# Raw second-layer weights loaded into the home of their low part and split there, one scratch for differences

## The chip, the cores and the metric

The kernel runs on one core of one Trainium2 chip. The metric is device time of one execution in microseconds (us), lower is better. TensorE (PE) multiplies, VectorE (DVE), ScalarE (ACT) and GpSimd (POOL) work on tiles in SBUF and on PSUM, and SyncE (SP) issues every DMA of this kernel in one queue, in the order of the program. Each engine takes its own instructions in order too; an instruction that waits holds all that stand behind it on its engine.

## What is computed

Three layers follow each other: causal attention with a decay, a gated layer with a layer norm (512 to 1024 to 512), and a squared-ReLU layer (512 to 2048 to 512). All is fp32.

```python
def reference(q, k, v, f, moe_w_in, moe_w_out, moe_g_ln, moe2_w_in, moe2_w_out):
    # batch 4, heads 8, tokens 576, head width 64
    cum = np.cumsum(np.log(np.clip(f, 1e-4, 1)), axis=-1)
    s = q @ k.T / 8 + cum[..., :, None] - cum[..., None, :]      # causal
    a = softmax(s) @ v
    x = a.reshape(2304, 512)
    h = x @ moe_w_in
    solu = h * softmax(h)
    x = (layernorm(solu) * moe_g_ln) @ moe_w_out
    h = np.maximum(x @ moe2_w_in, 0)
    return h * h @ moe2_w_out
```

## The kernel before

Products keep fp32 accuracy by splitting every operand into a high part (`hi`, rounded to fp32r) and a low part (`lo`, the difference), and running three matmuls: lo by hi, hi by lo, hi by hi. A split is one cast (`copy`, L376, L380 or L382 by engine: ACT, POOL, DVE) and one subtraction on DVE (`halves`, L1144).

Attention and the first layer take the time up to about 447 us of the profile. The second layer follows: tokens in blocks of 256, its 2048 hidden columns in eight pairs `p` of 256. A first block of 256 tokens is multiplied up by `half_up(p, ...)` (L1334), with weights `u0` to `u7` that `weightsh(p, ...)` loads and splits, into 32 homes `HU` of 128x512 (16 high, 16 low). All later blocks come in twos: `unit(b, p, ...)` (L1386) multiplies them up in seven products per pair (a Strassen scheme), and `step(blk, p, ...)` (L1487 to L1489) multiplies down, with weights of the second matrix that `weights2(p, ...)` loads and splits: per pair one piece of 256 columns (`a`) and three of 512 (`b`, `s`, `t`), each with a high and a low home. These homes are taken over from what the earlier stages leave: the first layer's weights `wih`, `wil`, `woh`, `wol`, the attention's `k1`, `k2`, `pt`, `e`, and small pieces of 256 (`ws`, `q3`, `qn`, `xc` and others). Many homes have two tenants in turn: `wil`, `k2`, `pt` and `e` hold weights of `half_up` first and weights of `step` afterwards.

Before the change, raw weights do not go to their homes. `load2` (L1158 to L1167) puts each into the next of six staging buffers `RAW` (`kn0`, `kn1`, `vn4`, `vn5`, `x`, `adj1`), and `halves` writes both parts into the homes. The same six buffers serve the token operands: `xload`, `xdiff` and `xsplit` of `x_block` (L1224, L1241, L1144) bring 512 tokens for the next units, and the last step of each block folds its output in them. The weights of the last pair come already split from DRAM (`w2s`, L1212).

A unit adds its products up with the help of a scratch of 128x256: it copies product 0 into it (`copy`), adds product 1, and then forms four sums from it (`add`, L1412). Before the change there are two scratches, `xw` and `maskb`, that units use in turn.

The order of all instructions is set by a planner, `Plan.lay`: each piece of work is a step with an engine, a cost, a priority (`prio`, a due time) and the buffer names that it reads and writes, and the planner lays them out as they become free. So a changed buffer changes the order on every engine. A load has the priority of its split less `AHEAD` (10 us). A home changes hands by `claim`, a step without cost that waits for the old tenant's last reader.

## Time and profile before

| | before |
|---|---|
| runs | 830.59, 824.18, 828.28 us; median 828.28 |
| profiled execution | 824.09 us, of it a span of 822.3 us |
| busy share of PE, DVE, ACT, POOL | 97%, 77%, 67%, 48% |
| DMA queue, share of 16 engines | 60.5% |

The profile is one execution. All times in the text are microseconds from the start of its span; 1.8 us of the execution lie around the span. A busy share is an average over the attention, the first and the second layer, which have different limits, so the stages are looked at one by one.

### The profile page before, as it was taken

The page shows a single profiled execution, that of the slowest core. Times are in us where ns is not written, and L with a number is a line of the kernel's source. Part 1 is how long each engine was busy: PE and PEld are TensorE (multiplying, and loading weights), DVE is VectorE, ACT ScalarE, POOL GpSimd, SP SyncE. Part 2 cuts the span into 40 slices and gives each one's busy share as a digit, 9 for nine tenths or more (in the row PEclk, how much of TensorE's full clock was granted, in tenths as well). Part 3 has the DMA queues.
Part 4 walks back from the last instruction along what each step waited for, and adds up shares of the span by engine and source line. Part 5 has one row for each costly group of instructions (what it writes and reads, how often), then busy time and mean ns, then how long its engine had stood idle before and what let it go on. Part 6 is the DMA issues. An engine that isn't in the chain of part 4 may idle for free.

```text
span 822.3 us, 19212 instructions
## 1 busy us (share of the span) xinstructions
PE 800.7 (97%) x6648; PEld 734.4 (89%) x6648; DVE 635.1 (77%) x1624; ACT 547.8 (67%) x1409; POOL 390.8 (48%) x539
## 2 busy tenths in 40 slices
PE   8899999999999999999999998999999999999997
PEld 7687777888888888888989998999999999999997
DVE  8898777878886667686658779779778867987776
ACT  6899988888797779899777676445335343533332
POOL 6467776767768777687777411021111121112110
PEclk9999999999999999999999999999999999999999
DMA  6643346657665554765557889896867767665401
GB/s 206 212 142 122 104 116 188 197 153 210 188 182 186 186 188 132 218 202 194 180 201 231 253 270 310 324 317 194 246 206 234 230 192 242 200 224 184 151 14 39
DMA packets 109665, 159.69 MB, mean 194 GB/s; under 512 B 12832, under 2 KB 52768, under 8 KB 109568
## 3 DMA queue, kind: packets, MB, share of 16 engines
q1 hardware_dynamic: 109568, 158.47, 60.5%
q8 instruction: 52, 0.85, 0.5%
q14 instruction: 45, 0.37, 0.2%
HBM read 121.65 MB, written 36.72 MB: 193 GB/s over the span
## 4 chain that ended last, share of the span: by engine, by line
PE 57%; ACT 3%; DVE 3%; issue 2%; DMA 1%; POOL 1%; DVEq 0%; POOLq 0%; ACTq 0%
PE pp L1386 9%; PE z L1386 9%; PE hp L1489 3%; PE hp L1488 3%; PE hp L1487 3%; PE z L1334 3%; PE pp L621 2%; PE z L567 2%; PE pp L811 2%; PE pp L812 2%; PE pp L813 2%; PE xo L641 2%; PE xo L1487 2%; PE xo L1489 2%; PE xo L1488 2%
## 5 line engine op out<-in xcount | busy, mean ns | idle before, releaser
L602 ACT ACTIVATE adj<-z,st 64x288 f32<-64x288 f32 (+9 forms) x192 | 95.1, 499 | 16.9 <-DVE st L588 15.9
L567 PE MATMUL z<-k,q 128*128 128x256 f32 (+17 forms) x384 | 90.0, 332 | 0.9 <-ACT adj L602 0.8
L588 DVE CUSTOM_DVE_ANT_0 z<-z,maskb 128x128 f32<-128x128 f32 (+8 forms) x144 | 65.2, 463 | 29.0 <-PE z L567 26.4
L621 PE MATMUL pp<-ident,adj 128*128 128x128 f32 (+1 forms) x480 | 76.6, 274 | 6.1 <-ACT adj L602 4.9
L812 PE MATMUL pp<-ln,wol 128*128 128x256 f32 x288 | 80.2, 278 | 0.0
L813 PE MATMUL pp<-ln,woh 128*128 128x256 f32 x288 | 80.1, 278 | 0.0
L1144 DVE TENSOR_TENSOR k<-adj,k 128x512 fp32r<-128x512 f32 x75 | 53.0, 706 | 33.8 <-POOL k L380 26.4
L376 ACT COPY pt<-pp 128x256 f32<-128x256 f32 (+5 forms) x169 | 67.2, 418 | 17.2 <-PE pp L621 16.1
L621 PEld LDWEIGHTS pp<-ident,adj 128*128 128x128 f32 (+1 forms) x480 | 50.6, 140 | 30.8 <-ACT adj L602 18.9
L380 POOL TENSOR_SCALAR k<-adj 128x512 fp32r<-128x512 f32 x39 | 24.3, 623 | 89.1 <-PE xo L1489 31.8
L734 POOL TENSOR_TENSOR free<-free 128x256 uint32<-128x256 uint32 x64 | 51.2, 807 | 31.0 <-DVE free L728 24.2
L567 PEld LDWEIGHTS z<-k,q 128*128 128x128 f32 (+3 forms) x384 | 54.9, 177 | 7.5 <-ACT adj L602 3.8
L641 PE MATMUL xo<-pt,vn 128*64 128x128 f32 (+1 forms) x960 | 61.1, 268 | 0.5 <-ACT pt L376 0.3
L860 PE MATMUL hp<-wih,xl 128*128 128x512 f32 x144 | 60.3, 419 | 0.8 <-ACT hp L899 0.8
L641 PEld LDWEIGHTS xo<-pt,vn 128*64 128x64 f32 x960 | 49.0, 137 | 11.3 <-issue 6.3
L861 PE MATMUL hp<-wil,xh 128*128 128x512 f32 x144 | 56.7, 394 | 0.2 <-DVE wil L738 0.2
L862 PE MATMUL hp<-wih,xh 128*128 128x512 f32 x144 | 56.7, 394 | 0.0
L812 PEld LDWEIGHTS pp<-ln,wol 128*128 128x128 f32 x288 | 54.4, 189 | 0.5
L813 PEld LDWEIGHTS pp<-ln,woh 128*128 128x128 f32 x288 | 54.2, 188 | 0.0
L1097 POOL TENSOR_TENSOR free<-free 128x256 f32<-128x256 f32 x64 | 52.5, 820 | 2.9 <-DMA w2f<-free 0.2
L1386 PE MATMUL z<-wol,k 128*128 128x256 f32 x384 | 52.5, 278 | 0.1
L1386 PE MATMUL pp<-wol,ln 128*128 128x256 f32 x384 | 51.9, 278 | 0.0
(597 smaller groups left out, 2686.3 us busy)
## 6 DMA issues: line engine op xcount, KB each, us to landing
k<-w2u SPq DMA_DIRECT2D x96, 256.0 KB
ln<-w2u SPq DMA_DIRECT2D x96, 256.0 KB
w2u<-free SPq DMA_DIRECT2D x56, 256.0 KB
kn<-in_k_dram SPq DMA_DIRECT2D x32, 256.0 KB
free<-in_moe_w_out_dram SPq DMA_DIRECT2D x32, 256.0 KB
free<-in_moe_w_in_dram SPq DMA_DIRECT2D x32, 256.0 KB
q<-w2u SPq DMA_DIRECT2D x32, 256.0 KB
w2f<-free SPq DMA_DIRECT2D x49, 128.0 KB
```

The lines of the kernel that those rows point to most:

```text
L376: nc.scalar.copy(dst(), src())
L567: nc.tensor.matmul(dst, lhsT=ql[0:r, p, 0:m], rhs=rhs, start=(g == 0), stop=(g == 1))
L588: nc.vector.tensor_tensor_reduce(out=z, in0=z, in1=maskb[0:m, o : o + e - a], scale=1.0, scalar=st[0:m, 0:1] if y else 3e38, op0=ALU.add, ...
L602: nc.scalar.activation(out=adj[0:m, c[1] : c[2]], in_=Z[c[0]][0:m, 0 : c[2] - c[1]], func=AF.Exp, bias=st[0:m, low : low + 1], scale=-1.0, ...
L621: nc.tensor.transpose(at(sk)[:, (c - g) * m : (c - g + 1) * m], adj[0:m, zc : zc + P], ident[0:m, 0:m])
L641: nc.tensor.matmul(XO[own[j], g // 2, off : off + m], lhsT=VN[vslot[b, c]][:, (g + j) * D : (g + j + 1) * D], rhs=PT[(s - h + g + j) % NPT ...
L812: nc.tensor.matmul(px, lhsT=wol[:, fc, w], rhs=hi, start=False, stop=False)
L813: nc.tensor.matmul(px, lhsT=woh[:, fc, w], rhs=hi, start=False, stop=(fc == KF - 1))
L860: nc.tensor.matmul(HP[:, c], lhsT=XL[i][:, cc, :], rhs=wih[:, cc, w], start=(cc == 0), stop=False)
L861: nc.tensor.matmul(HP[:, c], lhsT=XH[i][:, cc, :], rhs=wil[:, cc, w], start=False, stop=False)
L862: nc.tensor.matmul(HP[:, c], lhsT=XH[i][:, cc, :], rhs=wih[:, cc, w], start=False, stop=(cc == KC - 1))
L1386: nc.tensor.matmul(half(i), lhsT=l, rhs=r[:, c * TB : c * TB + TB], start=(j == start), stop=(j == 5), skip_group_check=True,)
```

## The change

Three things change. Each raw weight of the second layer is loaded into the home of its low part, cast from there into the home of its high part, and the low part is formed in place (`within` in the place of `load2` and the split); both homes are claimed 10 us of priority earlier, since the load needs one of them. The six staging buffers are left to the tokens and the outputs. `unit` has one scratch (`maskb`) in the place of two. The freed `xw` becomes the last small weight home, in the place of the end of `k11` (a last piece of 256 of `GS`), and its allocation stands a little earlier.

```diff
     new("q3", [640])
+    new("xw", [256])
...
     ident = new("ident", [P])
-    new("xw", [256])
...
-    GS = carve("k11", [512] * 5 + [256])
+    GS = carve("k11", [512] * 5)
...
-    small += GS[5:]
+    more("xw", 0, 1)
...
-    U2 = [carve(a, [256], F32)[0] for a in ("xw", "maskb")]
+    U2 = carve("maskb", [256], F32)[0]
...
-    turn = [0]
-
-    def load2(src, rk, n, prio):
-        ri = turn[0] % len(RAW)
-        turn[0] += 1
-        once(("raw", ri), RAW[ri], rk2(ri), prio)
+    def within(src, rk, hi, hk, lo, lk, n, prio):
 
         def fn():
-            dst = RAW[ri][0]()[:, 0:n]
+            dst = lo().bitcast(F32)
             nc.sync.dma_start(dst.rearrange("p (c x) -> p c x", x=256) if len(src.shape) == 3 else dst, src)
 
-        pl.add(dict(dma=LOAD2 * n / 512), fn, prio - AHEAD, rk, rk2(ri)[0 : n // 256])
-        return ri
+        pl.add(dict(dma=LOAD2 * n / 512), fn, prio - AHEAD, rk, [lk])
+        copy(n, hi, lambda: lo().bitcast(F32), prio, [lk], [hk], (), None, False)
+
+        def sub():
+            nc.vector.tensor_tensor(out=lo(), in0=lo().bitcast(F32), in1=hi().bitcast(F32), op=ALU.subtract)
+
+        pl.add(dict(dve=67 + 1.045 * n), sub, prio, [hk], [lk], port=True)
...
-                claim(HU[m], [hkeys[m]], prio)
+                claim(HU[m], [hkeys[m]], prio - AHEAD)
...
-                claim(W[nm + a], [("w2", p, nm + a)], prio)
+                claim(W[nm + a], [("w2", p, nm + a)], prio - AHEAD)
...
-        u2 = U2[n % 2]
-        uk = ("u2", n % 2)
-        once(uk, u2, [uk], prio)
+        uk = "u2"
+        once(uk, U2, [uk], prio)
```

In the order of instructions, lines of the changed kernel are two or three lower than before from L1170 on: `step` has L1484 to L1486, `unit` L1383, the adds to the scratch L1409. Its weight loads and weight splits are L1159 and L1165. The names give the tile that is written, the arrow what is read.

First the SP queue where the loads for `half_up` end. `w2d` are the raw weights of `half_up`, `w2f` those of `step`, `x2d` tokens. Before:

```order
L1164 DMA kn_50_4662<-w2d 128x512
L1164 DMA kn_50_4740<-w2d 128x512
L749 DMA w2d<-free_748 128x256
L1164 DMA vn_50_5380<-w2d 128x512
L1164 DMA vn_50_5425<-w2d 128x512
L749 DMA w2d<-free_748 128x256
L1164 DMA x_5434<-w2d 128x512
L1092 DMA w2u<-free_748 128x512
```

In the changed kernel:

```order
L1159 DMA pt_5396<-w2d 128x512
L1223 DMA kn_50_4673<-x2d 128x2x256
L749 DMA w2d<-free_748 128x256
L1223 DMA kn_50_4751<-x2d 128x2x256
L1159 DMA wil_5547<-w2d 128x512 x4
L749 DMA w2d<-free_748 128x256 x2
L837 DMA x2d<-xc_1416 128x256
L1092 DMA w2u<-free_748 128x512 x2
L1159 DMA wih_5648<-w2f 128x2x256 x3
```

The loads go to `pt` and `wil` now, the staging buffers `kn` take tokens, and four loads into `wil` stand together ahead of two stores of `w2d`.

Next DVE, where the splits of pair 4's weights (homes `wil`, after `half_up` is done with them) stand among the sums of the first two units and the split `k<-adj` that `step` of pair 2 reads. Before:

```order
L1144 TENSOR_TENSOR wil_5512<-vn_50_5425,wil_5512 128x512
L1412 TENSOR_TENSOR maskb_6172<-maskb_6172,pp_127 128x256
L1412 TENSOR_TENSOR ln1b_6082<-xw_6123,z_122 128x256 x2
L1144 TENSOR_TENSOR wil_5512<-adj_50_5282,wil_5512 128x512
L1144 TENSOR_TENSOR wil_5512<-kn_50_4662,wil_5512 128x512
L1412 TENSOR_TENSOR xl_50_5609<-maskb_6172,pp_125 128x256
L1412 TENSOR_TENSOR xl_50_5609<-xl_50_5609,pp_125 128x256
L1144 TENSOR_TENSOR wil_5512<-kn_50_4740,wil_5512 128x512
L1144 TENSOR_TENSOR k_50_5323<-adj_50_5620,k_50_5323 128x512
```

In the changed kernel:

```order
L1409 TENSOR_TENSOR maskb_6084<-maskb_6084,z_121 128x256
L1165 TENSOR_TENSOR woh_5909<-woh_5909 128x512
L1165 TENSOR_TENSOR wil_5547<-wil_5547 128x512
L1409 TENSOR_TENSOR ln1b_6072<-maskb_6084,z_122 128x256
L1409 TENSOR_TENSOR ln1b_6072<-ln1b_6072,z_122 128x256
L1165 TENSOR_TENSOR wil_5547<-wil_5547 128x512 x2
L1144 TENSOR_TENSOR ln1a_5939<-adj_50_5731,ln1a_5939 128x384
L1144 TENSOR_TENSOR k_50_5306<-adj_50_5667,k_50_5306 128x512
L1409 TENSOR_TENSOR ln1b_6072<-maskb_6084,z_122 128x256 x2
```

The splits of `wil` read no staging buffer any more. They still stand shortly ahead of `k<-adj`, and the second unit's sums in `maskb` stand behind the first unit's.

Last the SP queue where the loads of `step`'s weights end. Before:

```order
L1164 DMA kn_50_4662<-w2f 128x256
L1164 DMA kn_50_4740<-w2f 128x2x256
L1164 DMA x_5434<-w2f 128x256
L1164 DMA vn_50_5380<-w2f 128x2x256
L1164 DMA vn_50_5425<-w2f 128x2x256
L1164 DMA adj_50_5282<-w2f 128x2x256
L1164 DMA kn_50_4662<-w2f 128x2x256
L1164 DMA kn_50_4740<-w2f 128x2x256
L1164 DMA x_5434<-w2f 128x2x256
```

In the changed kernel:

```order
L1159 DMA woh_5909<-w2f 128x256
L1159 DMA free_5931<-w2f 128x2x256 x2
L837 DMA x2d<-xc_1416 128x256
L1159 DMA free_5931<-w2f 128x2x256
L1159 DMA woh_5909<-w2f 128x2x256 x4
L1372 DMA k_50_5306<-w2u 128x512
L1159 DMA wil_5547<-w2f 128x2x256 x3
L1372 DMA q_50_5367<-w2u 128x512
L1372 DMA ln_50_6088<-w2u 128x512 x3
```

Before, each load takes a staging buffer that an earlier load in the list had; now each goes to a home of its own.

## Rows read from the trace of the kernel before

**Rows 1.** The page's part 1: busy time, share of span, instructions.

```profile
PE 800.7 (97%) x6648; PEld 734.4 (89%) x6648; DVE 635.1 (77%) x1624; ACT 547.8 (67%) x1409; POOL 390.8 (48%) x539
```

**Rows 2.** Waits of PE over the span: total us, times, longest us.

```profile
PE pp L621 <- ACT adj L602: 4.9, 10, 1.3
PE xo L1487 <- DVE k L1144: 3.0, 2, 2.8
```

**Rows 3.** Stretches: length, busy PE, PEld, DVE, ACT, POOL; PE clock, DMA share, GB/s.

```profile
490.00:496.60 6.60, 6.60 (x57) 6.43 (x55) 6.09 (x14) 5.12 (x12) 0.00 (x0) 1.00 0.89 276
496.60:499.50 2.90, 0.15 (x3) 0.02 (x1) 2.38 (x6) 2.60 (x7) 0.62 (x1) 1.00 0.89 275
...
500.60:504.20 3.60, 3.60 (x20) 3.60 (x19) 2.87 (x9) 1.02 (x2) 1.92 (x2) 0.53 0.86 275
504.20:507.10 2.90, 2.61 (x21) 2.23 (x19) 2.46 (x6) 2.60 (x6) 0.17 (x1) 1.00 0.99 289
507.10:520.00 12.90, 12.90 (x108) 12.71 (x108) 11.35 (x32) 5.92 (x13) 0.00 (x0) 1.00 1.05 371
```

**Rows 4.** The chain that ended last, 491 to 500 us: start, us, what.

```profile
491.79 0.68 DVE woh L1144
...
492.50 4.83 DMA kn<-w2f
...
497.48 0.63 POOL wil L380
...
498.13 0.30 DVE wil L1144
...
498.74 0.70 DVE k L1144
...
499.48 0.38 PE xo L1487
```

**Rows 5.** Waits of the DMA queue (SPq), 440 to 510 us: total, times, longest.

```profile
SPq L1164 <- DVE q L1144: 3.9, 2, 2.7
SPq L1164 <- DVE k L1144: 3.8, 4, 1.8
SPq L1164 <- DVE wil L1144: 3.5, 4, 1.2
```

**Rows 6.** Timeline of PE: first layer's last read, then `half_up`'s first and last of `wil`.

```profile
442.33 0.40 PE L862 MATMUL hp<-wih,xh 128*128 128x512 f32 x1
...
450.74 0.88 PE L1334 MATMUL z<-vn,wil 128*128 128x256 f32 x6
...
452.14 2.32 PE L1334 MATMUL z<-vn,wil 128*128 128x256 f32 x18
...
468.93 0.88 PE L1334 MATMUL z<-vn,wil 128*128 128x256 f32 x6
```

**Rows 7.** Timelines of SP and ACT: a raw weight's load and its cast.

```profile
462.07 0.33 SPq L1164 DMA_DIRECT2D kn<-w2d  x1
...
465.74 0.62 ACT L376 CAST e<-kn 128x512 fp32r<-128x512 f32 x1 [2.32 <-DMA kn<-w2d]
```

**Rows 8.** Stretches as in rows 3, while the second layer's weights arrive.

```profile
440.00:460.00 20.00, 20.00 (x167) 19.61 (x166) 17.20 (x29) 15.68 (x35) 14.88 (x18) 1.00 0.78 244
460.00:480.00 20.00, 20.00 (x173) 20.00 (x173) 14.32 (x28) 12.43 (x29) 5.14 (x7) 1.00 0.81 255
```

**Rows 9.** The chain where two units start back to back: start, us, what.

```profile
570.71 2.84 PE pp L1386 x24
573.55 2.76 PE z L1386 x24
578.69 2.04 PE pp L1386 x18
585.49 2.04 PE z L1386 x18
```

**Rows 10.** Stretches as in rows 3, in the attention and first layer.

```profile
150.00:200.00 50.00, 49.78 (x402) 44.16 (x402) 38.61 (x106) 42.79 (x113) 35.93 (x48) 1.00 0.63 187
```

More of the change, by code (lines that the diff above doesn't have):

```diff
@@ L1174, in weightsh @@
         for c in range(2):
-            ri = load2(w2d[2 * p + c], [("w2d", 2 * p + c, z) for z in range(2)], 512, prio)
             for a in "hl":
@@ L1179, in weightsh @@
                 H2[p][f"u{c}{a}"] = HU[m]
-                claim(HU[m], [hkeys[m]], prio)
+                claim(HU[m], [hkeys[m]], prio - AHEAD)
             W = H2[p]
-            halves(
-                RAW[ri][0], rk2(ri), W[f"u{c}h"][0], ("w2", p, f"u{c}h"), W[f"u{c}l"][0], ("w2", p, f"u{c}l"), 512, prio
+            within(
+                w2d[2 * p + c], [("w2d", 2 * p + c, z) for z in range(2)],
+                W[f"u{c}h"][0], ("w2", p, f"u{c}h"), W[f"u{c}l"][0], ("w2", p, f"u{c}l"), 512, prio
             )
@@ L1199, in weights2 @@
                 W[nm + a] = again((small if n == 256 else large).pop(0))
-                claim(W[nm + a], [("w2", p, nm + a)], prio)
+                claim(W[nm + a], [("w2", p, nm + a)], prio - AHEAD)
             if p < KP - NPRE:
                 src = w2f[p, c[0]] if n == 256 else w2f[p, c[0] : c[0] + 2].rearrange("c p x -> p c x")
-                ri = load2(src, [("w2f", p, k) for k in c], n, prio)
-                halves(
-                    lambda ri=ri, n=n: RAW[ri][0]()[:, 0:n], rk2(ri)[0 : n // 256], W[nm + "h"][0], ("w2", p, nm + "h"),
+                within(
+                    src, [("w2f", p, k) for k in c], W[nm + "h"][0], ("w2", p, nm + "h"),
                     W[nm + "l"][0], ("w2", p, nm + "l"), n, prio,
@@ L1248, in x_half @@
             xsplit(g, 5 + g, prio)
-        turn[0] = 2
     def x_block(b, prio):
@@ L1352, in unit @@
         s1, s2 = (2 * b - 1, p), (2 * b, p)
-        u2 = U2[n % 2]
-        uk = ("u2", n % 2)
-        once(uk, u2, [uk], prio)
+        uk = "u2"
+        once(uk, U2, [uk], prio)
         def u2f():
-            return u2[0]()
+            return U2[0]()
         def half(i):
```

## The prediction

> **What bounds the kernel now.** I read the page's busy times first, then PE's waits, then the stretches in which they fall, the chain through the longest of them, and the waits of the DMA queue. PE is busy for 800.7 of the 822.3 us of the span [rows 1]. So 21.6 us of idle PE, and time lost to a low clock, are all that any change of order can win while the matmuls stay. PE's waits show where a piece of it lies that this change can reach: the waits of L621 on ACT belong to the attention, and the one long wait of the second layer is L1487 on the DVE split `k<-adj`, 2.8 us at its longest [rows 2]. In the stretches it stands at 496.6 to 499.5: PE is busy for 0.15 of 2.90 us [rows 3]. PE is full right before it (6.60 of 6.60) and from 507.1 on [rows 3].
>
> The chain says what was late there. The staging buffer `kn` is read by a split of `woh` from 491.79; as that ends, at 492.50, the next load into `kn` starts; it takes 4.83 us; POOL casts it (0.63), DVE subtracts for `wil` at 498.13, and only then comes DVE to `k<-adj` (0.70), for which PE starts at 499.48 [rows 4]. The weight in `wil` belongs to pair 4 and is not what PE wants; it merely stands ahead of pair 2's `k<-adj` on DVE. So the cause is a staging buffer that was free too late. The DMA queue shows the same from its side: weight loads wait for DVE splits that still read a staging buffer, 3.9, 3.8 and 3.5 us in the three longest groups [rows 5]. Meanwhile the DMA engines are not full: a share of 0.78 and 0.81 at 244 and 255 GB/s, against 1.05 and 371 GB/s at 507 to 520 [rows 8, 3].
>
> The gap has a price behind it. After it, PE's granted clock is 0.53 for 3.60 us, about the lower of its two levels (1.2 of 2.4 GHz), then back at 1.00 [rows 3].
>
> **The change part by part. Removed: the staging ring for weights.** What goes is the wait of a load on the split of an earlier load. Its worth is what PE lost: 2.90 - 0.15 = 2.75 us of gap, 3.60 x (1 - 0.53) = 1.69 us of low clock, and 2.90 - 2.61 = 0.29 us of the small wait behind it [rows 3], 4.73 us together. That all of it goes needs `wil`'s loads to be early by then. `half_up` reads `wil` last at 468.93, done at 469.81 [rows 6]; a load that then takes 4.83 us [rows 4] is there at 474.7, some 23 us before DVE came to it at 498.13 [rows 4]. In the new SP order these loads stand behind eight others into `woh` and `free`; at 256 KB each (2.1 MB) and the 255 GB/s of that time [rows 8] they take 8 us of the 23. In the order the splits of `wil` still stand ahead of `k<-adj`, so a late load would block DVE just as before; it is earliness alone that cures this.
>
> The work itself is the same: the same number of loads, of casts and of subtractions, at the prices of the old ones (0.63 for a cast, about 0.69 for a subtraction [rows 4]). That DVE reads and writes one tile costs no row anything; from both sides it lies between nothing and one more 0.69 per split, and I take nothing since the shape is the same.
>
> **Added: a load now waits for its home.** Before, a raw weight could lie in staging while its home was in use; now cast and subtraction wait for a load that starts only when the home is free. It matters where home and use are close together, at `wil`: PE reads the first layer's weights last at 442.33 + 0.40 = 442.73, and `half_up` wants `wil` at 450.74 and from 452.14 on [rows 6]. Four loads stand together. A raw weight took 465.74 - 462.07 = 3.67 us from the start of its issue to its cast [rows 7], 4.83 at the slowest [rows 4]; issues follow each other by about 0.4 (an issue takes 0.33 [rows 7]). So the first `wil` is there at 446.4 and split by 447.7. The third, with the casts one behind the other, is cast by 448.3 and split by 449.0; for the other work that ACT and DVE have there (15.68 and 17.20 of 20 us [rows 8]) I add the worth of two pieces, 1.3, which makes 450.3. The slack is 1.8 us against 452.14, and 0.6 with the slow load. I take nothing, and keep as the other end 3 us plus a clock dip of 1.69. The cover is PE's own work from 442.73 to 450.74, matmuls that need none of this.
>
> Here a rule of the Trainium skill speaks against the change. The page "Trainium Kernel Development and Optimization", section "Best Practices", says to double-buffer so that DMA overlaps with compute, and the change gives six staging buffers up. By that rule the loads at `wil` stand uncovered, and the time would be that of the second rival below; by the rows, other work of PE covers them, and the sum loses nothing.
>
> **Added: one scratch.** The second unit's copy waits until the first unit's last two sums are formed. Units mostly start after the one before has ended. Where two start back to back, the first (pp) has its second half from 578.69 to 580.73 and the next (z) its second half at 585.49 [rows 9]: 4.76 us for two sums, a copy and three sums. None of these is in my rows; the nearest is a split at twice the width, 0.69 [rows 4], and six of these make 4.1. It fits. There are six such places. Only at the first two units, near 485 to 495, does the new order bring the second unit's second half close behind the first's. I price this place at 0.4, between nothing and 1.4 (two pieces at 0.69).
>
> **Moved: three small splits** (`ws`, `q3`, `qn`) into the attention stage, since their homes are long free. Each has half the width of a split, so at most 0.63 + 0.69 us [rows 4], on ACT, POOL and DVE. By their neighbours in the order the first two fall into 150 to 200, where ACT and DVE work for 42.79 and 38.61 of 50 us and PE for 49.78 [rows 10]. Bounds: nothing, or the three in full, 4.0 us. PE there is bound by its own work, so I take 0.3; without that cover it would be the 4.0.
>
> **The sum.** 824.09 - 4.73 + 0.4 + 0.3 = 820.1 us against the profiled execution's 824.09, a change of -4.0. That execution is at the lower end of the runs (824.18 to 830.59); on the median of 828.28 the same change gives 824.2 us, 0.5% less. About 1% is what a measurement of this kernel can tell from no change.
>
> **First rival: the stall stays or only moves.** The four `wil` splits stand ahead of `k<-adj` still, and all loads go through one SP queue: if a load into `woh` waits for its home, the `wil` loads behind it wait too, and DVE again stands in front of PE. For it: the queue is in order, and DMA is full at 507 to 520 [rows 3]. Against it: from 440 to 480 there is a fifth of DMA left [rows 8]. It wins back nothing: 828.3 us, or 826 if only half of the 4.73 goes.
>
> **Second rival, on the other side: `wil` late for `half_up`.** Place: PE's L1334 on `wil` at 450.74 to 452.85. If the four loads land over 1.8 us later than priced, each further us is one of PE; and over some 2 us a clock dip of 1.69 is added, as behind the gap of 2.75 [rows 3]. It makes the kernel slower than before once it costs over 4.0, so at loads late by 1.8 + 2.3 = 4.1 us, which would be 7.8 us for a load. For it: the queue stands behind stores of `w2d` that wait for POOL; against it: neither load of the rows took over 4.83. At 6 us late: 824.2 + 4.2 + 1.7 = 830.1.
>
> **How the numbers follow.** Forecast 0.64: 824.2, its own range 820 to 827 with the scatter of medians. First rival 0.20: 826 to 829. Second rival 0.12: 828 to 834. The remaining 0.04 is for more, where PE's waits in the attention shrink with the new order: below 819. The range of 817 to 831 leaves out the far end of the second rival and some scatter. Over 1% faster is below 820.0: the last case and the low end of the forecast, 0.12. Over 1% slower is above 836.6: the far end of the second rival and a small part of the first, where the stall moves to a dearer place, 0.08. Within: 0.80.
>
> **What would show it.** Right: no PE wait on a DVE split near 497, no stretch at half clock up to 786, SP no longer waiting on DVE splits for weight loads, full PE from 440 to 500, and the units starting about 4 us earlier at equal work. The first rival shows as a wait of L1484 on `k<-adj` with a weight load behind it; the second as a wait of L1332 on a split of `wil` near 451. The scratch would show as a wait of L1383 on the copy into `maskb`, about 493; the small splits as more waits of L621 at 160 to 200. I am wrong if PE's busy time itself differs, or if the order's new sequence of units costs waits at places that were full.

## The result and the profile after

| | before | after |
|---|---|---|
| median of the runs beside each other | 825.53 us (823.82 to 830.59) | 816.48 us (815.5 to 821.4) |
| ratio, 95% interval | | 0.9889 [0.9852, 0.9926] |
| profiled execution, of it the span | 824.09, 822.3 us | 816.74, 814.9 us |

The change makes the kernel 1.1% faster (0.7 to 1.5% by the interval). The forecast was 824.2 us with a range of 817 to 831, so the gain is larger than forecast, and the time lies just below the range.

The page's part 1 of the changed kernel stands beside [rows 1]. PE's busy time itself fell by 4.2 us, with the same 6648 matmuls (the low clock that the sum priced at 1.69 us is in that, since PE counts as busy at it):

```profile
PE 796.5 (98%) x6648; PEld 730.9 (90%) x6648; DVE 636.8 (78%) x1626; ACT 544.4 (67%) x1405; POOL 392.2 (48%) x541
```

The waits of PE from 440 to 815 us (total us, times, longest) answer the second line of [rows 2]. The wait of `step` on `k<-adj` of 3.0 us is gone. The 0.7 that is left stands in the kernel before as well:

```profile
PE pp L1484 <- DVE k L1144: 0.7, 1, 0.7
```

The waits of the DMA queue from 440 to 510 us answer [rows 5]. Before, the longest group was a store (L749, held by POOL, 4.8 us), and the three next, those of [rows 5], were weight loads held by a DVE split. Now no weight load waits for a DVE split. One of the two longest groups is a weight load (L1159), for a home that PE still reads:

```profile
SPq L837 <- ACT xc L376: 4.3, 2, 3.1
SPq L1159 <- PE pp L938: 3.6, 1, 3.6
```

The stretches (columns as in [rows 3]) answer [rows 3, 8]. PE is full in every one, the clock is granted whole, and the transfers that were crowded behind the stall now come earlier: 365 GB/s at 480 to 500.

```profile
440.00:460.00 20.00, 20.00 (x163) 19.41 (x162) 15.87 (x30) 14.62 (x32) 13.04 (x15) 1.00 0.80 252
460.00:480.00 20.00, 20.00 (x175) 20.00 (x174) 15.27 (x29) 13.50 (x32) 6.06 (x8) 1.00 0.88 273
480.00:500.00 20.00, 20.00 (x177) 20.00 (x176) 17.83 (x34) 13.23 (x27) 5.82 (x8) 1.00 1.08 365
500.00:520.00 20.00, 20.00 (x177) 20.00 (x177) 15.41 (x43) 8.70 (x18) 1.75 (x3) 1.00 0.92 314
520.00:540.00 20.00, 20.00 (x178) 20.00 (x177) 15.21 (x42) 6.39 (x15) 4.13 (x7) 1.00 0.69 233
```

Two stretches of the kernel before show what these columns say beside the busy time. PE is busy for 20.00 of 20.00 us in both, at a clock of 1.00, but it starts 174 matmuls of the same size in the one and 179 in the other:

```profile
520.00:540.00 20.00, 20.00 (x174) 20.00 (x174) 14.85 (x42) 7.65 (x18) 2.36 (x4) 1.00 0.84 294
540.00:560.00 20.00, 20.00 (x179) 20.00 (x178) 15.92 (x39) 10.32 (x20) 4.16 (x6) 1.00 0.87 300
```

So there is a second piece of gain, inside busy time. The chain of the changed kernel where two units start back to back answers [rows 9], which had 2.84 and 2.76 us for the same 24 matmuls (`pp` and `z`). Here the 24 matmuls of the `pp` unit take 2.76:

```profile
564.53 2.76 PE pp L1383 x24
567.29 2.08 PE z L1383 x18
```

One measure carries the rest of this text: the time from PE's last start in the first layer (`hp<-wih,xh`, [rows 6]) to the start of the last unit's six `pp<-q` matmuls. Between the two lie the same matmuls in every kernel. From PE's timeline of before and, below it, of after:

```profile
782.03 0.88 PE L1386 MATMUL pp<-q 128*128 128x256 f32 x6
```

```profile
443.55 0.40 PE L862 MATMUL hp<-wih,xh 128*128 128x512 f32 x1
...
774.80 0.88 PE L1383 MATMUL pp<-q 128*128 128x256 f32 x6
```

That is 782.03 - 442.33 = 339.70 us before and 774.80 - 443.55 = 331.25 after. The attention and the first layer, which the change hardly touches, end between 442.3 and 444.3 in nearly all profiles with no relation to the edits, so the whole span says less than this difference does. Kernels for which no median is given below were run once, and have one profile.

| kernel | first layer's last read | last unit | between |
|---|---|---|---|
| before | 442.33 | 782.03 | 339.70 |
| before_again | 444.20 | 783.31 | 339.11 |
| e2_ring_one | 443.67 | 781.93 | 338.26 |
| e1_inplace_two | 442.98 | 776.65 | 333.67 |
| e4_tail_home | 443.73 | 777.43 | 333.70 |
| e5_head_home | 442.94 | 776.63 | 333.69 |
| e6_swap_home | 444.16 | 779.68 | 335.52 |
| e9_xw_above | 448.08 | 781.57 | 333.49 |
| e10_e_above | 443.63 | 776.38 | 332.75 |
| e7_wait_steady | 442.64 | 779.56 | 336.92 |
| e8_claim_late | 444.29 | 777.54 | 333.25 |
| after | 443.55 | 774.80 | 331.25 |
| after_again | 442.93 | 774.18 | 331.25 |
| e11_lower_above | 443.75 | 784.81 | 341.06 |
| e12_q_swap | 443.79 | 784.85 | 341.06 |
| e13_lower_z | 442.88 | 773.60 | 330.72 |
| e14_lower_pp | 443.79 | 774.75 | 330.96 |

### The profile page after: what moved, and what is told of

It reads as the page before. It is cut to its first block, busy times and chain, and to the rows that moved or that the text cites. A ratio compares the mean times of both kernels' runs of the same rounds, so it can differ in the third digit from the quotient of the medians.

```text
span 814.9 us, 19217 instructions
## 1 busy us (share of the span) xinstructions
PE 796.5 (98%) x6648; PEld 730.9 (90%) x6648; DVE 636.8 (78%) x1626; ACT 544.4 (67%) x1405; POOL 392.2 (48%) x541
## 4 chain that ended last, share of the span: by engine, by line
PE 56%; ACT 3%; DVE 3%; DMA 2%; issue 2%; POOL 1%; DVEq 0%; SPq 0%; POOLq 0%; ACTq 0%
PE z L1383 9%; PE pp L1383 9%; PE hp L1484 3%; PE hp L1486 3%; PE hp L1485 3%; PE z L1332 3%; PE pp L621 2%; PE pp L811 2%; PE z L567 2%; PE xo L1484 2%; PE xo L1486 2%; PE xo L1485 2%; PE pp L812 2%; PE pp L813 2%; PE hp L860 1%
## 5 line engine op out<-in xcount | busy, mean ns | idle before, releaser
L1144 DVE TENSOR_TENSOR k<-adj,k 128x512 fp32r<-128x512 f32 x72 | 50.5, 701 | 32.9 <-POOL k L380 24.9
L1383 PE MATMUL z<-wol,k 128*128 128x256 f32 x384 | 52.5, 276 | 0.0
L1089 POOL TENSOR_TENSOR free<-free 128x256 fp32r<-128x256 f32 x63 | 48.3, 781 | 8.4 <-ACT free L376 7.5
```

Source lines behind the costliest of these rows:

```text
L1383: nc.tensor.matmul(half(i), lhsT=l, rhs=r[:, c * TB : c * TB + TB], start=(j == start), stop=(j == 5), skip_group_check=True,)
```

## Experiments: which part of the change wins

No kernel below leaves out a part of the computation. Where a diff starts from the changed kernel, its minus lines are that kernel's; e2 starts from the kernel before.

**The kernel before once more, and the changed one once more.** Same files, to see the scatter of one profile.

> The kernel before, unchanged, profiled once more. If what the first profile showed belongs to the program, the gap near 497 us is 2.7 to 2.9 us again, the matmuls from 507 to 532 us stand 0.1175 us apart, and the slow stretches at pair 7 stand at the same places with 0.17 us each. If they are chance of one execution, they stand elsewhere or not at all.

The stall is there again, at `k<-adj` as in [rows 2], 2.4 us at its longest, and the measured stretch is 339.11 against 339.70.

> The changed kernel, unchanged, profiled and timed once more. If the pace belongs to the program, units start 16.36, 9.56 and 2.76 us apart again, with no stretch at 0.1175 us per matmul from 483 us on; the end of the first layer, 443.5 us in the first profile, may move by 1 to 2 us, as it did between two profiles of the kernel before (442.3 and 444.2).

The median is 815.97 us (815.19 to 817.59), the ratio 0.9892 [0.9858, 0.9927], and the stretch is 331.25 again. So differences of half a microsecond in this stretch between kernels can be read, as far as these two pairs go; in the kernels with the stall they can't quite. A short wait that comes in one kernel and not in another can cost more than that, as e8 and e9 show below, so it matters where in the stretch a difference lies.

**The ring alone taken away.** The changed kernel with two scratches and with the last small home back at the end of `k11`.

```diff
-    GS = carve("k11", [512] * 5)
+    GS = carve("k11", [512] * 5 + [256])
...
-    more("xw", 0, 1)
+    small += GS[5:]
...
-    U2 = carve("maskb", [256], F32)[0]
+    U2 = [carve(a, [256], F32)[0] for a in ("xw", "maskb")]
```

> The change's first part alone: weights are loaded into the home of their low part and split in place, but units keep two scratches in turn and the last small weight home stays at the end of k11. Theory A (the ring made the stall, the home at the end of k11 makes the slow stretches): no idle PE and no half clock between 485 and 510 us, and none of the long stretch at 0.1175 us per matmul that the kernel before shows from 488 to 532 us; but the stretches of some 43 matmuls at 0.1175 us in place of 0.1133 us that stand at pair 7 of each block of the kernel before (568 to 573 us, 607 to 612 us and so on, 0.17 us each) are still there, 6 or 7 of them, 1.0 to 1.2 us in all. Span 815.9 to 816.3 us against 814.9 of the changed kernel. Theory B (those stretches are left over from the disturbed start and go with the ring): 814.9 us and an even pace. Theory C (the scratch, not the ring, is what helps): a wait of 2 us or more near 497 us is left and the span is 820 us or more.

Measured: 818.64 us, ratio 0.9934 [0.9916, 0.9952], span 816.9, stretch 333.67. The stall and the low clock are gone; the ring alone (with the earlier claims, which e8 tests) is worth 339.4 - 333.67 = 5.7 us (339.4 is the mean of the two profiles of before). But pace is lost a little later. In two stretches of this kernel, PE starts 178 matmuls and then 169, with 0.06 us idle in the second:

```profile
500.00:520.00 20.00, 20.00 (x178) 20.00 (x177) 15.66 (x45) 7.40 (x17) 2.33 (x4) 1.00 0.92 312
520.00:540.00 20.00, 19.94 (x169) 19.73 (x168) 14.31 (x40) 8.03 (x18) 2.88 (x5) 1.00 0.75 249
```

The span is 0.6 to 1.0 us above what was expected: that stretch after the first pass of pair 7 was not foreseen.

**The ring kept, all the rest changed.** The kernel before with one scratch and the home in `xw`.

```diff
-    small += GS[5:]
+    more("xw", 0, 1)
...
-    U2 = [carve(a, [256], F32)[0] for a in ("xw", "maskb")]
+    U2 = carve("maskb", [256], F32)[0]
```

> The other two parts alone: the six staging buffers stay as in the kernel before, units have one scratch, xw is the last small weight home and stands a little lower. Theory A: the stall near 497 us stays with its low clock behind it and the slower pace of matmuls up to some 530 us; the slow stretches at pair 7 are gone, 1.0 to 1.2 us less than before: span 821.0 to 821.4 us. Theory B: stall and slow stretches both as before, 822.3 us. Theory C: no stall, below 818 us. The first units would show a wait on the copy into the one scratch near 490 us if the scratch costs what I took for it, 0.4 us.

Measured: 823.84 us, ratio 0.9994 [0.997, 1.0018], stretch 338.26. The wait of PE stands as before, with the lost pace behind it up to about 527. The low clock that was expected behind it did not come: the granted clock is 1.00 throughout, though the wait is longer (3.3 us against 2.8). Two waits near 504 and 506, 0.9 us each by the starts, are longer than in the kernel before instead. First the wait, then two stretches:

```profile
PE xo L1486 <- DVE k L1144: 3.9, 2, 3.3
```

```profile
500.00:520.00 20.00, 18.20 (x147) 17.59 (x148) 18.03 (x48) 11.39 (x24) 0.80 (x1) 1.00 0.94 329
520.00:540.00 20.00, 20.00 (x176) 20.00 (x175) 15.04 (x41) 8.58 (x19) 2.38 (x4) 1.00 0.86 303
```

So the two other edits are worth 1.1 us while the ring is there, and the ring is worth 338.26 - 331.25 = 7.0 with the other edits in. With e1 the pieces are not additive, and the next runs say why.

**The home alone put back.** The changed kernel, with the last small home at the end of `k11`.

```diff
-    GS = carve("k11", [512] * 5)
+    GS = carve("k11", [512] * 5 + [256])
...
-    more("xw", 0, 1)
+    small += GS[5:]
```

> The changed kernel with one thing undone: the last small weight home is the end of k11 again, and xw stays where it is but holds nothing. Theory A: the slow stretches at pair 7 come back, 1.0 to 1.2 us over the changed kernel, span about 816.0 us, with no other difference from 440 us on. Theory B: 814.9 us, pace of 0.1133 us per matmul throughout.

Measured: 819.62 us, ratio 0.994 [0.9912, 0.9968], stretch 333.70. Against e1 (333.67) the scratch costs 0.03 us, which is nothing. Against the changed kernel (331.25) the place of one home of 256 columns costs 2.45 us. PE's timeline shows where. Columns: start us, us, engine, line, out<-moving operand,stationary operand. This is pair 7's `step` in e4; the second row streams the weight from the end of `k11`:

```profile
562.06 0.28 PE L1484 MATMUL hp<-xc,ln1a 128*128 128x256 f32 x1
562.17 0.28 PE L1485 MATMUL hp<-k,ln1a 128*128 128x256 f32 x1
562.29 0.28 PE L1486 MATMUL hp<-xc,ln1a 128*128 128x256 f32 x1
562.41 0.28 PE L1484 MATMUL hp<-e,ln1a 128*128 128x256 f32 x1
```

And this is the same place in the changed kernel, with the weight in `xw`:

```profile
561.99 0.28 PE L1484 MATMUL hp<-xc,ln1a 128*128 128x256 f32 x1
562.10 0.28 PE L1485 MATMUL hp<-xw,ln1a 128*128 128x256 f32 x1
562.22 0.28 PE L1486 MATMUL hp<-xc,ln1a 128*128 128x256 f32 x1
```

A matmul of 256 columns starts 0.113 us after the one before. In e4, from the one that streams out of `k11` on, starts lie 0.1175 apart in the mean, and stay so for 51 or 63 matmuls, through the next unit (on `pp`) to the six `z<-q` of the unit behind it. The chain of e4 therefore has 2.84 us for the 24 matmuls of that `pp` unit, where the changed kernel has 2.76 (above):

```profile
566.11 2.84 PE pp L1383 x24
```

This costs 0.2 us per block. Six such blocks make 1.2. The other 1.2 lie in the block ahead of them, where the slower pace that begins with pair 7 at 521.9 lasts until about 547: 178 + 178 matmuls in 520 to 560 in the changed kernel against 170 + 176 in e4, 10 fewer at 0.113, which is 1.1. In that stretch PE also waits twice for DVE, too briefly for the list of waits (near 523.7 and 529.3, 0.38 us together). e1 and e5 have these waits too, the changed kernel has not; whether they prolong the slower pace is not shown. In e2 and in the kernel before, that stretch was slow anyway, behind the stall, so there the home is worth only the six blocks (1.15 measured). That is why the parts don't add up one by one.

## Experiments: what about the home

**The head of `k11` in place of its end.**

```diff
-    GS = carve("k11", [512] * 5)
+    GS = carve("k11", [256] + [512] * 5)
+    HEAD, GS = GS[:1], GS[1:]
...
-    more("xw", 0, 1)
+    small += HEAD
```

> The changed kernel with the last small weight home (pair 7's low part of 256 columns) at the beginning of k11 instead of in xw; the homes of the sums' high and low parts move up by one place in k11. Theory A1 (what matters is the place at the end of k11): the even pace of the changed kernel, 16.36 and 2.76 us from unit to unit, span about 815 us. Theory A2 (what matters is that the weight shares k11 with operands that DVE, ACT and POOL write all the time): slow stretches at pair 7 as with the end of k11, 2.84 in place of 2.76 us from a unit to the next there, 2.5 us more than the changed kernel, span about 817.5 us.

Measured: span 816.9, stretch 333.69, with the same slower pace at pair 7. It is not the end of that tile, nor a tile's last bytes.

**The low part of pair 3 there in place of pair 7's.**

```diff
-    GS = carve("k11", [512] * 5)
+    GS = carve("k11", [512] * 5 + [256])
...
-    more("xw", 0, 1)
+    small.append(small[7])
+    small[7] = GS[5]
```

> The changed kernel with two small weight homes exchanged: the end of k11 holds pair 3's low part, the third piece of ws holds pair 7's. Theory A1 or A2 (the home is what matters): the slow stretches move to pair 3 of each block and are gone at pair 7; their length and price there (0.2 to 1.2 us a block) depend on what resets the pace. Theory A3 (pair 7's place in the order matters, whatever its home): they stay at pair 7, 0.18 us each.

Measured: span 820.4, stretch 335.52. The slower pace moves with the home: it begins in pair 3's `step` now, pair 7 is even, and it lasts longer (0.44 us a block). In the chain of e6 the first `pp` unit of this row lies behind pair 3, and the second begins as the slower pace has ended:

```profile
586.33 2.84 PE pp L1384 x24
...
596.24 2.76 PE z L1384 x24
```

**`xw` kept as the home, but allocated where it stood before.** The order of instructions is that of the changed kernel on every engine; only the addresses differ.

```diff
-    new("xw", [256])
     ADJ = [new(f"adj{i}", [AW]) for i in reversed(range(NADJ))][::-1]
...
     ident = new("ident", [P])
+    new("xw", [256])
```

> The changed kernel with one thing undone: xw is allocated where it stood before, 12.7 KB higher in each partition; the order of instructions is the same on every engine. Theory P (a matmul pays when its moving operand lies in the same upper part of the memory as the stationary operands k10, k11, ln0, ln1a): if that part begins below 170 KB, slow stretches at pair 7 as with the end of k11, 2.84 in place of 2.76 us there and 9.65 in place of 9.56, 1.3 to 2.5 us more than the changed kernel. Theory A2 (sharing the tile k11 is what matters): the even pace of the changed kernel, 16.36 and 2.76 us, the same time from 444 us on.

Measured: stretch 333.49, 2.24 us more than the changed kernel, with one allocation moved and no instruction. The chain shows pair 7's unit at 2.84 again:

```profile
570.25 2.84 PE pp L1383 x24
```

But only 1.3 of the 2.24 us lie at pair 7, where `step` reads `xw` seven times in the stretch, at 0.17 to 0.23 each. The other 0.9 were lost before the first of these reads. From PE's timeline, a start that comes 0.14 us late, and the first read of `xw`:

```profile
498.49 0.28 PE L1486 MATMUL hp<-wih,ln1a 128*128 128x256 f32 x1
498.74 0.97 PE L1383 MATMUL pp<-wol,ln 128*128 128x256 f32 x6
...
529.31 0.28 PE L1485 MATMUL hp<-xw,ln1a 128*128 128x256 f32 x1
```

There PE waits for a sum on DVE, and behind it the slower pace holds until 518. Neither profile of the changed kernel has this wait, though the order is the same; e10 and e8, below, have it. DVE's split `ln1a<-adj` shortly before takes 0.97 us in e8, e9 and e10 and 0.55 in the changed kernel; why is open, and since e8 leaves all addresses as they are, the place of `xw` is not shown to be the cause. So the address is worth 1.3 us here, and that the whole comes near the 2.45 of e4 is chance.

(The whole span was 821.4, since in this profile PE's clock was granted at 0.93 over 100 to 200, in the attention, and the first layer ended at 448.08; this is why only the second layer is compared.)

In the program as built, `xw` lies at byte 158,144 of each partition in the changed kernel and at 170,880 in e9; `k11`, where the other kernels have the home, begins at 193,408. The stationary operands of `step` lie above 180,000 (`ln1a` at 216,960, `k10` at 182,144), and two other homes that it streams from lie lower (`wil` at 18,880, `e` at 121,792). The tiles allocated between the two places of `xw` move down by its 1,024 bytes in e9; in e10, below, those between move by 4,096.

**`e` allocated above.** `e` is a home of four weights; it moves from 121,792 to 200,576, and the order is again the same.

```diff
-    E = new("e", [DF])
     q2 = new("q2", [2, 2, HH, P], F32R)
...
     K1 = [new(f"k1{j}", [HH, KW], F32R) for j in range(2)]
+    E = new("e", [DF])
```

> The changed kernel with the tile e (stationary weights of half_up, then moving weights of the last pairs' step) allocated above k11 instead of between pt and q2; the order of instructions is the same on every engine. Theory P: half_up's matmuls on e, which take 0.120 us each in both kernels while those on k10 take 0.113, come down to 0.113 (12 of them, 0.08 us), and step's matmuls on e at pair 7 now start slow stretches of 0.1 to 0.4 us a block. Theory A2: nothing changes, half_up on e 0.120, 16.36 and 2.76 us from unit to unit.

Measured: span 816.7, stretch 332.75, 1.5 us more: 1.3 of it is the slower pace at pair 7 again, in seven places (`step` streams from `e` there), and 0.25 a wait near 494 like that of e9, which set no slower pace here. But `half_up`, which has its weights as the stationary operand, became faster on `e`. A row of six lasts five spacings and one matmul's own 0.28, so 0.88 us are spacings of 0.12, and 0.84 are 0.113. The changed kernel's timeline first, then that of e10, where `e` is fast and its neighbour `pt` is not:

```profile
480.93 0.88 PE L1332 MATMUL z<-vn,e 128*128 128x256 f32 x6
```

```profile
481.02 0.84 PE L1332 MATMUL z<-vn,e 128*128 128x256 f32 x6
...
481.70 0.88 PE L1332 MATMUL z<-vn,pt 128*128 128x256 f32 x6
```

So in the second layer, two operands on the same side cost pace: both low, each matmul takes 0.12; both high, the pace falls to 0.1175 and stays there for a while. A low moving and a high stationary operand run at 0.113. "Side" is only a name for what these addresses do: low is up to 158,144 for the moving operand and up to 125,888 for the stationary one, high from 170,880 and, with e11 below, from 173,952. A high moving and a low stationary operand do not meet in this layer.

## Experiments: waits and claims

**A wait put where there was none.** The changed kernel, with one DVE split of block 3, pair 3 (512 columns) done nine times, so that PE has to wait for it in an even stretch.

```diff
-            nc.vector.tensor_tensor(out=lo(), in0=raw(), in1=hi().bitcast(F32), op=ALU.subtract)
+            for _ in range(times):
+                nc.vector.tensor_tensor(out=lo(), in0=raw(), in1=hi().bitcast(F32), op=ALU.subtract)
...
-        halves(blocks(sx, 0, 4), [xk, yk], hi["S"][0], ("gh", g, "S"), lo["S"][0], ("gl", g, "S"), 512, prio)
+        halves(blocks(sx, 0, 4), [xk, yk], hi["S"][0], ("gh", g, "S"), lo["S"][0], ("gl", g, "S"), 512, prio, (), 9 if (blk, p) == (3, 3) else 1)
```

> The changed kernel with one split drawn out: the subtraction for the low part of the sums of block 3, pair 3 (near 620 us) is done nine times over, the same result each time, 8 x 0.62 = 5.0 us more of DVE; it is done some 3.5 us before PE wants it. So PE waits about 1.5 us there, perhaps again for the adds behind it. Theory W (a wait of PE starts the slow pace): behind the wait the matmuls stand 0.1175 us apart for tens of matmuls, 0.2 to 1.3 us on top of the wait. Theory O (only certain operands do): 0.1133 us at once after the wait; the cost is the wait alone, and a low clock if the granted clock falls.

Measured: stretch 336.92, 5.67 us more. The wait was 3.7 us, more than the 1.5 that was meant:

```profile
PE z L1384 <- DVE q L1410: 3.7, 1, 3.7
```

A low clock stands behind the wait, as behind the stall of the kernel before [rows 3], though none stood behind the 3.3 us of e2: granted 0.94 and 0.63 in the two stretches after the wait's begin, and whole again from 626 on:

```profile
618.00:622.00 4.00, 1.03 (x7) 1.03 (x8) 3.90 (x10) 0.05 (x1) 0.00 (x0) 0.94 0.23 66
622.00:626.00 4.00, 4.00 (x24) 4.00 (x24) 4.00 (x10) 1.21 (x4) 0.51 (x1) 0.63 0.46 131
626.00:630.00 4.00, 4.00 (x37) 4.00 (x36) 3.03 (x9) 3.07 (x7) 1.80 (x3) 1.00 0.33 85
```

At 622 to 626, 24 matmuls start where 35 would at 0.113: 1.2 us. The 2.0 us that the wait cost beyond its own 3.7 are thus of the kind and size of the 1.69 in the prediction. The slower pace behind it lasted only from 624.95 to 626.6.

**The early claim undone.** Homes claimed at the priority of the split again.

```diff
-                claim(HU[m], [hkeys[m]], prio - AHEAD)
+                claim(HU[m], [hkeys[m]], prio)
...
-                claim(W[nm + a], [("w2", p, nm + a)], prio - AHEAD)
+                claim(W[nm + a], [("w2", p, nm + a)], prio)
```

> The changed kernel with the homes claimed at the priority of the split, as before, not 10 us earlier. Theory A: the homes are long free and the claim costs no engine anything, so loads move little: within 1 us of the changed kernel from 440 us on, no wait of PE on a split. Rival: the loads wait for their claims, weights come late again and a wait of PE of 1 us or more stands between 445 and 530 us.

Measured: span 817.7, stretch 333.25, 2.0 us more, which is beyond theory A's 1 us, and no new wait of PE in the list of waits, so the rival did not come either. A single delay of 0.1 us shows in its timeline, and then a different pace: the six `pp<-wol` at 494.82 take 0.80 us to the next start, where six take 0.68.

```profile
494.70 0.28 PE L1486 MATMUL hp<-wih,ln1a 128*128 128x256 f32 x1
494.82 0.96 PE L1383 MATMUL pp<-wol,ln 128*128 128x256 f32 x6
495.62 0.28 PE L1484 MATMUL xo<-free,k 128*128 128x256 f32 x1
```

From there until 515 starts lie 0.1175 apart, then the pace is even again:

```profile
495.00:515.00 20.00, 20.00 (x171) 20.00 (x171) 17.71 (x45) 9.96 (x21) 1.93 (x3) 1.00 0.96 332
515.00:525.00 10.00, 10.00 (x90) 10.00 (x89) 6.40 (x18) 4.35 (x10) 1.30 (x3) 1.00 0.83 266
```

Two more short waits, near 525.0 and 530.6 (0.06 and 0.34 us), have the slower pace behind them until about 548. So a delay that is too short to see as a wait can set the slower pace too, and the first one here costs 0.7 us of pace for 0.1 of delay. That the later claim brings these waits is not shown: e9 and e10 have the first of them with the claim early.

## Experiments: can the six matmuls on `q` be won too

In the changed kernel, six matmuls of each unit (`pp<-q` or `z<-q`) have both operands in `q2` (byte 125,888) and run at 0.12 ([rows 9] has them inside its groups). What I expected to win is 6 x 0.0067 us x 32 units, 1.3 us.

**The stationary one of the two moved above.** `q2` becomes two tiles, and the units' first stationary operand goes to `q100` and `q101`, which lie higher.

```diff
-    c = carve("q2", [512] * 4)
-    lower, XOP[0] = c[:2], c[2:]
+    lower, XOP[0] = [carve(f"q10{j}", [512])[0] for j in range(2)], carve("q21", [512] * 2)
```

> The changed kernel with one exchange of homes: each unit's first stationary weights, which lie in the lower half of q2 (about 126 KB up in each partition) beside the tokens that they meet, lie in q100 and q101 (174 KB up) instead, and two of the ten places for results take their room; q2 is allocated as two tiles for it, so the order differs a little. Theory P (a matmul is slower when both operands lie on the same side of the memory): the six matmuls of each unit on q2, 0.120 us each in every kernel so far, come down to 0.113; 32 x 6 x 0.0067 = 1.3 us less than the changed kernel, 9.52 us in place of 9.56 from one unit to the next, span 812.6 to 813.7. If sides are not what matters: 0.120 us still, 813.9 to 814.9.

Measured: 826.68 us, ratio 1.0021 [1.0001, 1.0042], stretch 341.06, 9.8 us more than the changed kernel. The six matmuls did become fast (0.84 per six at 487.84, where 0.88 stood). But a delay of about 0.1 us at 494.86 set the slower pace, and it never ended: 342 matmuls in 40 us, up to the end of the kernel, where the changed kernel starts 353 and e13, below, 355:

```profile
560.00:600.00 40.00, 40.00 (x342) 40.00 (x341) 30.72 (x86) 14.48 (x30) 6.82 (x12) 1.00 0.68 212
```

**The same with `q1` and `q2` exchanged in the allocation.** The attention has `q1` and `q2` as operands too.

```diff
-    Q2 = [[q2[:, i, j] for j in range(2)] for i in range(2)]
+    Q1 = [[new(f"q1{i}{j}", [HH, P], F32R) for j in range(2)] for i in range(2)]
...
-    Q1 = [[new(f"q1{i}{j}", [HH, P], F32R) for j in range(2)] for i in range(2)]
+    q2 = [new(f"q2{i}", [2, HH, P], F32R) for i in range(2)]
```

> As the run before, and beyond it the attention's stationary operands change sides: q1 is allocated where q2 stood and q2 where q1 stood, so that k1 (upper part) meets q1 (now lower) and k2 (lower) meets q2 (now upper). Units as in the run before. Theory P: the attention's 384 score matmuls lose what the same side costs them, by the 0.0067 us of the second layer 2.6 us of PE; a part of it is lost to waits on ACT, so 1 to 2.5 us less up to the end of the first layer, near 441.5 us, span 810 to 813. If sides are not what matters: the first layer ends at 442.9 to 443.6 us as in the two profiles of the changed kernel.

Measured: 826.98 us, ratio 1.0019 [1.0004, 1.0035]. The second layer is e11's (341.06). The first layer ends at 443.79, as elsewhere, so in the attention the sides make no difference that shows. That end scatters by 2 us, as much as was expected to be won, so this says little.

**Only the units on `z`, only the units on `pp`.** Half of the units keep their six matmuls in `q2`.

```diff
-    c = carve("q2", [512] * 4)
-    lower, XOP[0] = c[:2], c[2:]
+    lower, XOP[0] = [carve("q100", [512])[0], carve("q201", [512])[0]], [carve(f"q21{j}", [512])[0] for j in range(2)]
```

> As the run with lower moved up (e11_lower_above), but for the units on z alone: their first stationary weights lie in q100, those of the units on pp stay in q2, where they meet tokens of q2. The order of instructions is that of e11_lower_above. Theory R (a short delay sets the slower pace of 0.1175 us, and the six matmuls of a unit with both operands in q2 are what sets it back): the slow stretch that begins near 495 us ends at the q2 matmuls of one of the next units on pp, within 60 us, and the rest is even; units on z take 0.04 us less each, 0.6 us in all: span 813.5 to 815.5. If the slow pace has another cause that came with the exchange of homes: 342 matmuls in 40 us to the end as in e11_lower_above, span 825.

Measured: 816.49 us, ratio 0.9914 [0.9885, 0.9942], stretch 330.72, 0.53 less than the changed kernel; 16 units at 6 x 0.0067 would be 0.64. A start at 494.04 comes 0.09 us late, but the slow stretch that was expected behind it did not come, so this run does not test theory R. The pace is even all along:

```profile
560.00:600.00 40.00, 40.00 (x355) 40.00 (x354) 30.44 (x85) 14.25 (x30) 7.40 (x13) 1.00 0.67 214
```

> The other half: the units on pp have their first stationary weights in q101, those on z keep theirs in q2. Theory R: as in the run before, with the slow stretch ending at the q2 matmuls of a unit on z; span 813.5 to 815.5. Otherwise 825. If only one of the two runs gets its pace back, it is not the q2 matmuls as such that set it back, but what stands around them in that kind of unit.

e14 is the reverse of e13 (`q200` and `q101`). Measured: 816.51 us, ratio 0.9899 [0.988, 0.9918], stretch 330.96. Here the slower pace came at 494.95, as in e11, and it ended at the first unit that still has both operands in `q2`, as theory R has it. From its timeline:

```profile
494.95 1.67 PE L1383 MATMUL pp<-vn,ln 128*128 128x256 f32 x12
...
500.45 0.88 PE L1383 MATMUL z<-q,q 128*128 128x256 f32 x6
```

So the six slow matmuls, at 0.04 us a unit, also do something: every end of the slower pace that I found lies at such a group (532.3 before, 596.3 in e6, 626.6 in e7, 500.45 in e14), though not every group ends it (507.3, 519.9 and 526.0 before did not), and without any (e11, e12) it had no end. e13 and e14 are level with the changed kernel within their intervals; neither is a faster kernel that I can show.

## Why the prediction was wrong, point by point

**What bounds the kernel, and the removed stall: right in kind, its size too small.** The stall's place, its cause (a staging buffer that came free too late) and its cure hold: no PE wait near 497, no low clock, and SP no longer waits for DVE with weight loads. The term was 4.73 us; the ring alone measured 5.7 (before to e1). What is missing is in PE's timeline of before, in waits that I did not add up because they are short and PE counts as busy in them. Two of the places, three starts each; an even pace would have 0.23 us from the first to the third, and there are 0.58 and 0.48:

```profile
487.54 0.28 PE L1489 MATMUL hp<-free,ln1a 128*128 128x256 f32 x1
487.89 0.39 PE L1386 MATMUL z<-wol,k 128*128 128x256 f32 x1
488.12 0.88 PE L1386 MATMUL z<-q 128*128 128x256 f32 x6
...
513.45 0.28 PE L1489 MATMUL hp<-k,ln1a 128*128 128x256 f32 x1
513.71 0.39 PE L1487 MATMUL xo<-k,k 128*128 128x256 f32 x1
513.93 0.28 PE L1488 MATMUL xo<-k,k 128*128 128x256 f32 x1
```

These two cost 0.35 and 0.25 us. With those at 504.9 (0.56) and 506.9 (0.23) they make 1.4 us, of which I had counted 0.29. All of them are gone. 4.73 + 1.1 = 5.8 against the 5.7 of e1.

All starts of the measured stretch together say the same. I add up what each 256-column matmul starts later than 0.1133 us after the one before, apart for starts over 0.125 us apart (waits and low clock) and under it (pace):

| kernel | waits and low clock | pace |
|---|---|---|
| before | 6.3 | 4.5 |
| e1_inplace_two | 0.5 | 4.3 |
| after | 0.1 | 2.3 |

The first column is what the ring took away; the second is the next point. About 2.2 us of the pace stand in each of the three, at matmuls with both operands in `q2` or in `half_up`.

**The last small home: the step that failed.** The part on what is added and moved has no term for it. I read `xw` in the place of the end of `k11` as a rename and priced nothing, not even a bound. It is worth 2.45 us in the changed kernel (e4 to after; e5 2.44). Of that, 1.3 us is shown to be the address: e9 and e10, with the order of the changed kernel, lose as much at pair 7. The remaining 1.1 us is the long slow stretch from 521.9 to 547, which came in e1, e4 and e5 with the home in `k11` and not in e9; what prolongs it is open. The rows had it: [rows 9] shows 2.84 us and 2.76 us for the same 24 matmuls, and I used these rows for the scratch without asking why they differ. "I am wrong if PE's busy time itself differs" was the sentence that came true, 800.7 to 796.5. The sentence that idle PE and a low clock "are all that any change of order can win" was the mistake behind it: full PE stood at two paces.

**One scratch: nothing.** Priced at 0.4, measured at 0.03 (e1 to e4). No wait of L1383 on the copy into `maskb` is in the list of waits. The place was not far off: the short waits of e8, e9 and e10 near 494 to 498 are L1383 waiting for a sum into `maskb`. e1, with two scratches, and e4, with one, both lack them, so no run tells whether the one scratch has a part in them.

**The small splits that moved early: not seen.** Priced at 0.3. The first layer ends at 443.55 and 442.93 in the two profiles of after, at 442.33 and 444.20 in those of before, and at 443.67 in e2, which does not move them. The scatter of 2 us is wider than the term.

**The loads at `wil` (second rival): did not come.** PE is full from 440 to 460. On DVE, the last two splits of `wil` end at 451.06 + 1.30 = 452.36, and PE's timeline (below the DVE row) reads `wil` first at 451.95 and in its long group from 453.35 on, so about 1.0 us of slack is left where I had 1.8:

```profile
451.06 1.30 DVE L1165 TENSOR_TENSOR wil<-wil 128x512 fp32r<-128x512 f32 x2 [0.16 <-POOL wil L380]
```

```profile
451.95 0.88 PE L1332 MATMUL z<-vn,wil 128*128 128x256 f32 x6
...
453.35 0.88 PE L1332 MATMUL z<-vn,wil 128*128 128x256 f32 x6
```

The rule on double buffers in the Trainium skill ("Trainium Kernel Development and Optimization", section "Best Practices") would have had these loads uncovered; the trace does not bear that out here. A home that is free early enough does what a staging buffer would. The low clock that this rival adds behind a wait is not sure to come either: e2 has a wait of 3.3 us without it.

**The stall stays (first rival): no.** The splits of `wil` still stand ahead of `k<-adj` on DVE, but their loads are there in time.

**The anchor.** The sum was -4.0 us, 820.1 on the profiled execution. I set it on the median of three runs, 828.28, which was high: medians of the kernel before beside the later runs are 825.53, 824.47, 824.71, 824.63 and 824.42. So of the 7.7 us between 824.2 and 816.5, about 4.2 are the anchor (828.28 - 824.09) and the rest is size: in the second layer 8.15 us were gained (339.4 to 331.25), twice the sum. The sum lacks the home (2.45) and the short waits (1.1), and the 0.7 that it adds for the scratch and the small splits did not show. With the right anchor the forecast would still have been some 3.6 us too high.

## What to carry to other kernels

Count the instructions per stretch beside the busy time: where an engine is full at 174 matmuls in 20 us here and 179 there, there is gain inside "full", and a chain that shows two durations for the same work shows the place. When a change gives a tile another address, price it by such rows, with a run that moves only the allocation where it matters. When a stall goes, add up the short gaps around it by starts and not by busy time, and set the sum on the profiled execution when three runs scatter by 6 us.

## What the runs showed of the hardware that I had not expected

The spacing of PE's matmuls (256 columns, fp32r, clock 1.00) in the second layer depends on where its operands lie in the partition: 0.113 us with the moving operand low and the stationary one from 173,952 up; 0.12 with both low (`half_up` on `e`: 0.88 per six, and 0.84 with `e` at 200,576); and with both high (`k11`, `xw` at 170,880, `e` at 200,576) a pace of 0.1175, which stays after the operand is gone, for 51 matmuls and more (up to 25 us in e4, with two short waits in it). Between 158,144 and 170,880 the moving operand changes sides. The same pace was set by delays of about 0.1 us (e8, e11, e14) and behind the stall, though not by every delay: 0.09 in e13 and 0.25 in e10 left no mark.

A low clock behind a wait of PE was no sure thing: the waits of 2.8 us in before, 2.4 in before_again and 3.7 in e7 had granted clocks of 0.53, 0.66 and 0.63 over 3.6, 5 and 4 us behind them, and the 3.3 us of e2 had 1.00.

The Trainium skill says in "TensorE: Matmul & The Clock Gate", section "Step-by-step: what each phase is for", that PE has two independent read ports, one for the streamed operand and one for the weight load, so that loading the next weights takes no read bandwidth from the running matmul. No run here looks at the ports themselves. What the runs show is not what that sentence leads one to expect: e9 and e10 change nothing but where tiles lie, and the pace changes by 4 to 6% (0.1133 to 0.1175 and 0.12). The measurement decides, for this layer; in the attention e12 showed no effect beyond its scatter.

What stays open: what holds the slower pace, why it ends at groups with both operands in `q2` and not at each of them, what makes the short waits near 494 to 498 come in some kernels and not in others, and where exactly between the two addresses of `xw` the side changes. None of this was tried further.
